# A linear-attention and GEGLU block on one core: M's high part and a chunk's parts of q in places that lie idle in the second pass, the sum of phi(k) by two fp32r products, and an order of instructions searched anew

## The chip, the cores and the metric

The kernel runs on one core of one Trainium2 chip. The core has five engines that work side by side: TensorE (PE, with its weight loads shown as PEld), VectorE (DVE), ScalarE (ACT), GpSimd (POOL) and SyncE (SP), which issues the transfers (DMA). Each engine takes its own instructions strictly in the order in which they were written down for it, and waits where an operand is not there yet. The metric is the time of one execution in device microseconds, where less is better.

## The reference

With x of 2048 rows (tokens) and 512 columns, 32 heads of 16 columns, and F = 1792:

```python
xn = layernorm(x)
q, k, v = xn @ wqkv, by heads
phi = lambda t: where(t > 0, t + 1, exp(t)) + 1e-6
kv  = einsum("bhsd,bhse->bhde", phi(k), v)
z   = einsum("bhsd->bhd", phi(k))                 # the sum of phi(k) over the tokens
o   = einsum(phi(q), kv) / (einsum(phi(q), z) + 1e-6)
s   = o @ wo
g   = silu((gelu(xn @ w_gate) * (xn @ w_up)) @ w_down)
out = x + s * g
```

All inputs and outputs are fp32.

## The kernel before

**Arithmetic.** An fp32 operand is split into a high part, rounded to the type fp32r, and a low part, which is the rest (`split`, L644: ACT casts the high part, DVE subtracts). A product of two split matrices is then three TensorE products, high by high, high by low and low by high (`three`, L671). The large matrix products are also taken apart by the Strassen-Winograd scheme: seven products of half-size blocks, gathered in three PSUM banks X, Y and Z. Product 1 is made in X and copied to Y by ACT (the "seed"), product 2 is added to Y; products 6, 7 and 4 are added to X, products 5 and 3 to Z. Between two of them a bank is saved or read by ACT or DVE, so a product has to wait until the one before it has been copied. Such a place, where PE makes a product, ACT copies it and PE goes on from the copy, is called a hand-over below. Almost every TensorE instruction is a 128x128 by 128x512 matmul that passes through one line, L665.

**Stages.** The tokens form four chunks of 512, taken in the order 2, 3, 0, 1.

- First stage, some 135 us: layernorm of 16 blocks of x, their transposes (`pt`, L866), the products for k and q (`k`, `q`, `X`, `Y`, `Z`), phi(k), its product with xn (`gps`), and its sum over the tokens (`zacc`, added up on POOL). k, q and phi are turned and spilled to DRAM.
- Then the sum of phi(k) over the partitions of `zacc` (`pz`, L1149, one fp32 product with a matrix of ones, named blk in the profile), kv (L1203) and the matrix M = kv times wo for all heads (L1210), which goes to DRAM as a high and a low part (`m_d`).
- The gated part runs in two passes over the weights, 28 weight tiles `w` each: pass 1 for the tokens of chunks 2 and 3, pass 0 (the second) for chunks 0 and 1. A weight tile gives three banks `FX`, `FY`, `FZ` (`quad`); their results go through gelu and the product with the up part into `h` and its split parts `hfh`, `hfl`; the down product gathers in banks `dX`, `dY`, `dZ` (`down_strassen`) and is added to `acc`. In the second pass the weight tiles come back from DRAM (1792 KB each) into three places of a ring (`ring("w", ...)`).
- At the turn from the first pass to the second, near 345 us, the attention products of chunk 2 are made (`sps`) and put aside in DRAM (`s_d`), silu is taken of the four first-pass sums, the tokens' split parts `Xh` and `Xl` are exchanged (14 transfers of 512 KB), and the weight tiles of the second pass begin to come in.
- End: the products of phi(q) with M for chunk 3 (the first end chunk, mixed with the last down products), then of chunks 0 and 1 (`sps`), the product with silu(g), the sum with x, and the transfers out.

**Where M and phi(q) lie at the end.** `load_m` takes two places of the weight ring, M0 (high) and M1 (low), 1024 KB each, when the weight tiles there are done with. phi(q) comes from DRAM into the places of `Xh` and `Xl` (the pool "xf", halves named pqh and pql): chunk 3 into pql, chunk 0 into pqh, chunk 1 into pql again. For chunk 3 the high and low parts were already split and stored (`t_d`, `tl_d`), so 8 transfers of 256 KB bring them in. pql becomes free when the last product of the last weight tile that reads `Xl` is done.

**The order.** The program is first noted down as operations with their costs and their predecessors (class `Plan`). TensorE's operations have a rough order, a list of keys (`pe_keys`), from which they may step ahead by 6 us at most. `Plan.order` (L309) then gives every operation a time by which it has to be done (`late`); `forward` (L440) runs through a model of the engines, and at each step gives an engine the ready operation with the lowest `late`. What comes out is the order of each engine's queue, for all five engines. Before, `late` comes from eight rounds of a backward reckoning (`latest`), followed by a list of random alterations that were kept (`KEPT`, `altered`).

Matmuls of 512 columns follow each other at a steady step when nothing is waited for; the rows of the prediction show it.

Of the kernel before, what the change touches and what calls it, by code (L numbers as in the profile page):

```python
# [18 lines left out]
KEPT = [  # L19
    (55, 70, [720000004]),  # L20
    (115, 135, [720000005]),
    (200, 270, [720000009]),
    (500, 560, [720000027]),
    (-1, 12, [720000035]),
    (70, 85, [720000040]),
    (-1, 12, [720000043]),
    (25, 40, [720000085, 720000134]),
    (200, 270, [720000140]),
    (-1, 12, [720000144]),
    (200, 270, [720000152]),  # L30
    (340, 420, [720000172, 720000184]),
    (100, 115, [720000203]),
    (340, 420, [720000233]),
    (500, 560, [720000243]),
    (40, 55, [720000247]),
    (560, 605, [720000257]),
    (200, 270, [720000279]),
    (340, 420, [720000290]),
    (500, 560, [720000362]),
    (200, 270, [720000390]),  # L40
    (55, 70, [720000517]),
    (40, 55, [720000540]),
    (340, 420, [720000555]),
    (270, 340, [720000602, 720000649, 720000655]),
    (340, 420, [720000658]),
    (270, 340, [720000690]),
    (500, 560, [720000887]),
    (12, 25, [720000899]),
    (55, 70, [720000957]),
    (500, 560, [720000974]),  # L50
    (40, 55, [720001218]),
    (-1, 12, [720001311]),
    (25, 40, [720001456]),
    (115, 135, [720001543]),
    (40, 55, [720001818]),
    (25, 40, [720001887]),
    (85, 100, [720001895]),
    (135, 200, [720001949]),
    (340, 420, [720002052]),
    (500, 560, [720002094]),  # L60
    (115, 135, [720002310]),
    (100, 115, [720002326]),
    (500, 560, [720002367]),
    (135, 200, [720002396]),
    (40, 55, [720002422]),
    (270, 340, [720002472]),
    (200, 270, [720002488]),
    (55, 70, [720002565, 720002605]),
    (115, 135, [720002669]),
    (100, 115, [720002694]),  # L70
    (55, 70, [720002734]),
    (40, 55, [720002796]),
    (100, 115, [720002858]),
    (40, 55, [720002901]),
    (340, 420, [720002982]),
    (70, 85, [720003200]),
    (420, 500, [720003430]),
    (-1, 12, [720003440]),
    (40, 55, [720003709, 720003813]),
    (70, 85, [720003981]),  # L80
    (115, 135, [720004064]),
    (25, 40, [720004170]),
    (100, 115, [720004402]),
    (500, 560, [720004624, 720004745]),
    (420, 500, [720004920]),
    (340, 420, [720005018]),
    (420, 500, [720005191]),
    (500, 560, [720005291]),
    (340, 420, [720005364]),
    (270, 340, [720005386]),  # L90
    (500, 560, [720005573]),
    (270, 340, [720005617]),
    (500, 560, [720005700, 720005753, 720005812]),
    (70, 85, [720005857]),
    (100, 115, [720005876, 720006137]),
    (200, 270, [720006523]),
    (340, 420, [720006542]),
    (270, 340, [720006565]),
    (500, 560, [720006740]),
    (270, 340, [720006762]),  # L100
    (420, 500, [720006797]),
    (100, 115, [720006937]),
    (25, 40, [720007069]),
    (100, 115, [720007820]),
    (270, 340, [720007916]),
    (200, 270, [720007997]),
    (100, 115, [720008028]),
    (40, 55, [720008434]),
    (70, 85, [720008559]),
    (40, 55, [720008706]),  # L110
    (55, 70, [720008751]),
    (-1, 12, [720008785, 720010301]),
    (25, 40, [720011151]),
    (-1, 12, [720011236]),
    (500, 560, [720011560]),
    (340, 420, [720011716]),
    (270, 340, [720011832]),
    (55, 70, [720011869, 720011995]),
    (40, 55, [720012578, 720013114]),
    (135, 200, [720013435]),  # L120
    (12, 25, [720013929]),
    (270, 340, [720014337]),
    (70, 85, [720015269]),
    (340, 420, [720015275]),
    (12, 25, [720015459]),
    (340, 420, [720016007]),
    (55, 70, [720016730]),
    (100, 115, [720016972]),
    (40, 55, [720017118]),
    (420, 500, [720019299, 720019742]),  # L130
    (25, 40, [720023341]),
    (560, 605, [720025689]),
    (200, 270, [720026707, 720027204]),
    (500, 560, [720027907]),
    (200, 270, [720029093]),
    (270, 340, [720029251]),
    (200, 270, [720030011]),
    (135, 200, [720030869]),
    (500, 560, [720031562]),
    (25, 40, [720032237]),  # L140
    (70, 85, [720033404]),
    (500, 560, [720034357]),
    (70, 85, [720034379]),
    (55, 70, [720034598]),
    (135, 200, [720037606]),
    (70, 85, [720037790, 720038397]),
    (200, 270, [720038864, 720039585]),
    (270, 340, [720041466]),
    (340, 420, [720041524]),
    (270, 340, [720041782]),  # L150
    (340, 420, [720043687]),
    (270, 340, [720043952]),
    (500, 560, [720044378]),
    (420, 500, [720044730]),
    (500, 560, [720044844]),
    (55, 70, [720045169]),
    (340, 420, [720045191]),
    (500, 560, [720045753]),
    (420, 500, [720045914]),
    (40, 55, [720046385]),  # L160
    (270, 340, [720047033]),
    (500, 560, [720047485]),
    (340, 420, [720048926]),
    (500, 560, [720049727]),
    (340, 420, [720050930, 720051286]),
    (500, 560, [720053709]),
    (420, 500, [720054380]),
    (70, 85, [720054716]),
    (135, 200, [720055100]),
    (500, 560, [720057087, 720057360, 720057458, 720057584, 720058015, 720058243]),  # L170
    (70, 85, [720058559]),
    (500, 560, [720059111, 720061740, 720062259]),
    (420, 500, [720065756]),
    (500, 560, [720067854, 720081154, 720082022]),
    (340, 420, [720085320]),
    (500, 560, [720089253]),
    (200, 270, [720097314]),
    (500, 560, [720110408, 720110529, 720112057, 720115333]),
    (200, 270, [720127077]),
    (420, 500, [720127080]),  # L180
    (40, 55, [720140141, 720140280, 720140297, 720140482]),
    (115, 135, [720140633]),
    (55, 70, [720141777]),
    (100, 115, [720141903]),
    (40, 55, [720144894]),
    (25, 40, [720146503]),
    (55, 70, [720146889]),
    (70, 85, [720147845]),
    (40, 55, [720149073]),
    (55, 70, [720163394, 720163465, 720163560, 720163641, 720163851]),  # L190
    (270, 340, [720165618]),
    (500, 560, [720168148, 720168524, 720169268, 720170070, 720170695]),
    (25, 40, [720171786]),
    (500, 560, [720172318]),
# [65 lines left out]
class Plan:  # L260
# [48 lines left out]
    def order(self, pe_keys):  # L309
        rank = {k: i for i, k in enumerate(pe_keys)}  # L310
        pe = sorted((o for o in self.ops if o.eng == "PE"), key=lambda o: rank[o.key])
        now = 0.0
        for o in pe:
            o.turn = now
            now += o.cost
        best = None
        done = self.ops_in_turn(pe)

        for n in range(8):
            self.latest(done, now, capacity=n > 0)  # L320
            done = self.forward(pe)
            end = max(t for t, _ in done)
            if best is None or end < best[0]:
                best = end, done, {o: o.late for o in self.ops}
# [7 lines left out]
    def altered(self, n, lo, hi, pe, _, done, late):  # L332
        draw = random.Random(n)
        for o in self.ops:
            o.late = late[o]
        waits = [w for w in self.waits(done) if lo <= w[0] < hi]
        if not waits or draw.random() < 0.3:
            waits += [(o.turn, 0.1, o) for o in pe if lo <= o.turn < hi]
        if not waits:
            return _, done, late  # L340
        w = draw.choices(waits, [w[1] for w in waits])[0]
        if draw.random() < 0.5:
            for o in self.chain(done, w[2]):
                if draw.random() < 0.7:
                    o.late -= draw.uniform(0.0, 4.0)
        else:
            at, back = w[2].late, draw.uniform(1.0, 12.0)
            share, far = draw.choice((1, 2, 3, 0.05, 0.2, 0.5)), draw.uniform(0.2, 4.0)
            near = [o for o in self.ops if at - back < o.late < at + 2.0]
            for o in draw.sample(near, min(len(near), share)) if share >= 1 else near:  # L350
                if share >= 1 or draw.random() < share:
                    o.late += draw.uniform(-far, far)
# [16 lines left out]
    def chain(self, done, o):  # L369
# [9 lines left out]
        for _ in range(14):  # L379
# [4 lines left out]
            if not held:  # L384
                break
# [1260 lines left out]
```

## Time and profile before

| | |
|---|---|
| median of 3 runs | 602.98 us (602.73 to 603.38) |
| the profiled execution's own time | 602.79 us |
| its span | 601.1 us |
| PE busy | 593.4 us (99%), 2626 matmuls |
| PEld (weight loads) busy | 481.2 us (80%) |
| DVE, ACT, POOL busy | 83%, 61%, 40% |
| granted TensorE clock | full in every slice |
| DMA | 141.27 MB, mean 235 GB/s |

The profiled execution is 0.19 us below the median, and its span is 1.69 us shorter than its time. A profile row gives a start in us from the span's start, a duration, the engine, the line, the operation, out<-in, and how many instructions the row stands for; square brackets hold the idle time of the engine ahead of the row and what ended it. The ends of matmuls are modelled, so PE looks busy in a row longer than a matmul's step; what a matmul really takes is read from the starts of those that follow.

### The profile page before, as it was taken

The page shows a single profiled execution, that of the slowest core. Times are in us where ns is not written, and L with a number is a line of the kernel's source. Part 1 is how long each engine was busy: PE and PEld are TensorE (multiplying, and loading weights), DVE is VectorE, ACT ScalarE, POOL GpSimd, SP SyncE. Part 2 cuts the span into 40 slices and gives each one's busy share as a digit, 9 for nine tenths or more (in the row PEclk, how much of TensorE's full clock was granted, in tenths as well). Part 3 has the DMA queues.
Part 4 walks back from the last instruction along what each step waited for, and adds up shares of the span by engine and source line. Part 5 has one row for each costly group of instructions (what it writes and reads, how often), then busy time and mean ns, then how long its engine had stood idle before and what let it go on. Part 6 is the DMA issues. An engine that isn't in the chain of part 4 may idle for free.

```text
span 601.1 us, 7826 instructions
## 1 busy us (share of the span) xinstructions
PE 593.4 (99%) x2626; PEld 481.2 (80%) x2626; DVE 499.3 (83%) x768; ACT 367.4 (61%) x663; POOL 242.0 (40%) x237
## 2 busy tenths in 40 slices
PE   8999999999999999999999999999999999999997
PEld 6887788777878888888887788888888888887786
DVE  6999988988788989999877675757698889898887
ACT  6687778877677765655545469567454544545620
POOL 4455856847636763605043730521122221206000
PEclk9999999999999999999999999999999999999999
DMA  7149977758986245467975899944656566648967
GB/s 271 46 131 281 287 229 237 235 186 275 379 314 226 91 158 209 158 210 299 336 231 184 323 393 381 332 163 140 210 174 210 175 228 201 218 156 269 364 219 269
DMA packets 78807, 141.27 MB, mean 235 GB/s; under 512 B 4656, under 2 KB 47664, under 8 KB 74672
## 3 DMA queue, kind: packets, MB, share of 16 engines
q1 hardware_dynamic: 78768, 140.79, 67.9%
q8 instruction: 20, 0.33, 0.2%
q14 instruction: 19, 0.16, 0.1%
HBM read 87.82 MB, written 52.95 MB: 234 GB/s over the span
## 4 chain that ended last, share of the span: by engine, by line
PE 85%; DVE 6%; DMA 6%; issue 1%; ACT 1%; SPq 0%; ACTq 0%; DVEq 0%
PE FX L665 25%; PE FZ L665 13%; PE dX L665 12%; PE FY L665 6%; PE gps L665 6%; PE dY L665 6%; PE X L665 4%; PE dZ L665 3%; DMA g<-g_d 2%; PE Z L665 2%; PE q L665 2%; PE sps L665 2%; PE k L665 2%; DMA pqh<-t_d 1%; PE Y L665 1%
## 5 line engine op out<-in xcount | busy, mean ns | idle before, releaser
L665 PE MATMUL FX<-Xh,w 128*128 128x512 f32 x448 | 134.7, 391 | 0.0
L1374 POOL TENSOR_TENSOR h<-h,g 128x512 f32<-128x512 f32 x28 | 38.9, 1390 | 150.5 <-DVE h L638 150.2
L665 PEld LDWEIGHTS FX<-Xh,w 128*128 128x128 f32 x448 | 83.9, 188 | 18.2 <-ACT fu L632 0.4
L665 PE MATMUL FX<-Xl,w 128*128 128x512 f32 x224 | 68.8, 389 | 0.0
L665 PE MATMUL FZ<-Xh,w 128*128 128x512 f32 x224 | 68.3, 391 | 0.0
L632 ACT COPY fu<-FX 128x512 f32<-128x512 f32 x56 | 32.9, 587 | 45.7 <-PE FX L665 43.2
L632 ACT COPY dY<-dX 128x512 f32<-128x512 f32 x56 | 32.0, 571 | 40.0 <-DVE acc L1328 30.6
L632 ACT CAST hfh<-sums 128x512 fp32r<-128x512 f32 x56 | 34.7, 622 | 27.9 <-DVE sums L638 27.7
L665 PEld LDWEIGHTS FZ<-Xh,w 128*128 128x128 f32 x224 | 42.0, 188 | 9.2 <-issue 0.5
L665 PEld LDWEIGHTS FX<-Xl,w 128*128 128x128 f32 x224 | 42.0, 188 | 8.8
L665 PE MATMUL dX<-hfh,dh 128*128 128x512 f32 x112 | 43.8, 395 | 0.3 <-ACT dY L632 0.3
L665 PE MATMUL dX<-hfl,dh 128*128 128x512 f32 x112 | 43.6, 391 | 0.0
L638 POOL TENSOR_TENSOR tmp<-raw 128x256 f32<-128x256 f32 x28 | 24.6, 886 | 47.2 <-ACT fu L632 24.1
L665 PE MATMUL dX<-hfh,dl 128*128 128x512 f32 x112 | 43.5, 390 | 0.0
L1328 DVE TENSOR_TENSOR acc<-acc,dX 128x512 f32<-128x512 f32 x48 | 32.9, 685 | 11.3 <-PE dX L665 10.7
L638 DVE TENSOR_TENSOR hfl<-sums,hfh 128x512 fp32r<-128x512 f32 x56 | 39.9, 721 | 2.5 <-ACT hfh L632 1.7
L1328 DVE TENSOR_TENSOR acc<-acc,dY 128x512 f32<-128x512 f32 x48 | 32.8, 684 | 10.8 <-PE dY L665 10.6
L638 POOL TENSOR_TENSOR sums<-draw 128x256 f32<-128x256 f32 x28 | 23.5, 850 | 34.9 <-DMA draw<-in_B_w_down 26.1
L638 DVE TENSOR_TENSOR hfl<-h,hfh 128x512 fp32r<-128x512 f32 x42 | 34.1, 817 | 1.6 <-ACT hfh L632 1.6
L638 DVE TENSOR_TENSOR h<-fu,FZ 128x512 f32<-128x512 f32 x28 | 19.2, 687 | 18.4 <-ACT fu L632 13.3
L665 PE MATMUL FY<-Xh,w 128*128 128x512 f32 x112 | 34.5, 390 | 0.0
L665 PE MATMUL FZ<-Xl,w 128*128 128x512 f32 x112 | 34.3, 389 | 0.0
(205 smaller groups left out, 1513.5 us busy)
## 6 DMA issues: line engine op xcount, KB each, us to landing
w<-w_d SPq DMA_DIRECT2D x17, 1792.0 KB, 7.9
w_d<-w SPq DMA_DIRECT2D x11, 1792.0 KB, 8.1
draw<-in_B_w_down SPq DMA_DIRECT2D x14, 512.0 KB, 6.4
w_d<-we SPq DMA_DIRECT2D x18, 256.0 KB, 2.1
x<-in_A_x SPq DMA_DIRECT2D x16, 256.0 KB, 4.5
q_d<-qp SPq DMA_DIRECT2D x16, 256.0 KB, 3.0
qz<-q_d SPq DMA_DIRECT2D x16, 256.0 KB, 3.7
q<-q_d SPq DMA_DIRECT2D x16, 256.0 KB, 3.9
```

The lines of the kernel that those rows point to most:

```text
L632: do("ACT", act(n, src.psum), lambda o, i: nc.scalar.copy(o, i), dst, src, name=name)
L638: do(eng, c, lambda o, p, q: getattr(e, f"tensor_{op}")(o, p, q), dst, a, b, name=name)
L665: nc.tensor.matmul(o if r is None else o[:, r], a, b, start=first, stop=made == self.passes[r], skip_group_check=self.on or r is not None)
L1328: do("DVE", dve(D), lambda o, i: nc.vector.tensor_add(o, o, i), o, ps, name="acc")
L1374: do("POOL", pool(NC), lambda o, i: nc.gpsimd.tensor_mul(o, o, i), h, g, name="h")
```

## The change

The change has four parts.

1. The sum of phi(k). `zacc` is split into two fp32r parts (an ACT cast and a DVE subtraction, 128x512 each), the matrix of ones is cast to fp32r once (128x128, ACT, at the very start), and `pz` is made of two fp32r products, ones by z's high part and ones by its low part, in place of one fp32 product.
2. M's high part. `load_m_early` takes it as two tiles Mh of 512 KB in the places R0 and R1 of the pool "rawp", which held raw weights and phi(q) of chunk 2 in the first pass and nothing in the second. The two transfers stand at the turn of the passes. The low part (Ml, 1024 KB) stays in the weight ring, one place of the ring earlier.
3. The parts of phi(q) of chunk 3. Seven of the eight go into one place of the weight ring (`pqw`), the eighth into a small idle tile (`pqt`, the place TMP of "rawp"). Chunk 0 takes the whole of pql, chunk 1 the whole of pqh.
4. The order. `latest`, `altered` and `KEPT` are gone; `late` is a table of numbers, one per operation (`LATE`), and `forward` makes the order from it as before.

```diff
-KEPT = [
-    (55, 70, [720000004]),
...
+LATE = [
+    -22047, 38, -946, 3475, -22738, -54555, -46091, -264, -48805, 868, 403, 695, 109, 1778, 1311, 1344, 1773, 1633, 154,
...
@@ Plan.order
-        best = None
-        done = self.ops_in_turn(pe)
-        for n in range(8):
-            self.latest(done, now, capacity=n > 0)
-            done = self.forward(pe)
...
-        for lo, hi, draws in KEPT:
-            for n in draws:
-                best = self.altered(n, lo, hi, pe, *best)
-        return [o for _, o in best[1]]
+        for o, late in zip(self.ops, LATE, strict=True):
+            o.late, o.lat0 = late / 100, o.lat
+        return [o for _, o in self.forward(pe)]
...
     pz = bank(7, "pz")
-    do("PE", 0.9, lambda o, a, b: nc.tensor.matmul(o, a, b, start=True, stop=True), pz, ones, zacc, key="z")
+    ones_r = tile_in("sm", "onr", [P, P], F32R, "ones_r")
+    do("ACT", 0.2, lambda o, i: nc.scalar.copy(o, i), ones_r, ones, name="ones")
+    zs = [tile_in("up", n, [P, D], F32R, f"z{n}") for n in (29, 32)]
+    split(*zs, zacc, D, "z")
+    def run_z(o, a, *zs):
+        for n, z in enumerate(zs):
+            nc.tensor.matmul(o, a, z, start=n == 0, stop=n == 1)
+    do("PE", 2 * PASS, run_z, pz, ones_r, *zs, key="z")
...
-            M.append(m)
+            M.append(lambda k, rows, m=m: m[:, k, rows])
         return M
+    def load_m_early():
+        high = [tile_in("rawp", r, [P, 2, D], F32R, f"Mh{r}") for r in (R0, R1)]
+        for r, m in enumerate(high):
+            src = View([m_d(k, ()).res[0] for k in (2 * r, 2 * r + 1)], m_d(0, (0, slice(None), slice(2 * r, 2 * r + 2))).get)
+            dma(m.map(lambda ap: ap.bitcast(F32)), src, 512)
+        low = tile_in("wp", ring("w", [0, 1, 2]), [P, KT, D], F32R, "Ml")
+        src = View([m_d(KT + k, ()).res[0] for k in range(KT)], m_d(KT, 1).get)
+        dma(low.map(lambda ap: ap.bitcast(F32)), src, 1024)
+        return [lambda k, rows: high[k // 2][:, k % 2, rows], lambda k, rows: low[:, k, rows]]
...
     keys, wait = ffn(0, moved)
-    M = load_m()
+    M = load_m_early()
+    pq = [tile_in("wp", ring("w", [0, 1, 2]), [P, 7, D], F32R, "pqw", 7), tile_in("rawp", TMP, [P, 2, D], F32R, "pqt", 1)]
     vs = {hl: tile_in("xf", hl, [P, 14, NC], F32R, f"pq{hl}", 14) for hl in "lh"}
...
-    for c, hl in zip(CHUNKS[1:], "lhl"):
+    attn(CHUNKS[1], M, lambda i, n: pq[(i - KT) // 7].part(
+        pq[(i - KT) // 7].res[(i - KT) % 7:(i - KT) % 7 + 1], (slice(None), slice((i - KT) % 7, (i - KT) % 7 + 1))))
+    for c, hl in zip(CHUNKS[2:], "lh"):
         attn(c, M, lambda i, n, v=vs[hl]: v.part(v.res[i:i + n], (slice(None), slice(i, i + n))))
```

How the rows stand in the queues, at three places. A row has the line, the operation, out<-in with each tile's number, the shape, and the count of equal instructions in a row (x4). The line numbers of the changed kernel are lower, since code was taken out ahead: L513 is there what L628 is before (the DMA issue), and L550 what L665 is (the matmul).

The SP queue (DMA issues) at the end, before: `M_5301` is M's low part, `draw` a raw down weight, `pql` the parts of phi(q) of chunk 3 from `t_d` (high) and `tl_d` (low), then `pqh` of chunk 0, `sxr` x for the last sum, `g` the silu of a first-pass sum, `s` what was put aside of chunk 2.

```order
L628 DMA sxr_5223<-in_A_xT 128x512
L628 DMA t_d<-sums_3674 128x4x128
L628 DMA draw_6_5284<-in_B_w_down 128x2x512
L628 DMA M_5301<-m_d 128x2048
L628 DMA s_5322<-s_d 128x512
L628 DMA g_5346<-g_d 128x512
L628 DMA g_5358<-g_d 128x512
L628 DMA pql<-t_d 128x512 x4
L628 DMA pql<-tl_d 128x512 x4
L628 DMA pqh<-t_d 128x4x512
L628 DMA s_5406<-s_d 128x512
```

And after:

```order
L513 DMA t_d<-sums_3702 128x4x128 x2
L513 DMA Ml<-m_d 128x2048
L513 DMA sxr_5248<-in_A_xT 128x512
L513 DMA draw_6_5276<-in_B_w_down 128x2x512
L513 DMA pqw<-t_d 128x512 x4
L513 DMA pqw<-tl_d 128x512 x3
L513 DMA s_5346<-s_d 128x512
L513 DMA g_5368<-g_d 128x512
L513 DMA g_5379<-g_d 128x512
L513 DMA s_5395<-s_d 128x512
L513 DMA pqh<-t_d 128x4x512
```

Here `pqh` is of chunk 1. The seven pieces for chunk 3 now stand right behind the last raw down weight, ahead of `s` and both `g`; the eighth (`pqt`) was issued some twenty rows earlier.

The same queue at the turn of the passes, before: `w_3451`, `w_3635` and `w_3657` are the second pass's first three weight tiles, numbered w14, w15 and w16 below, `so` the products of chunk 2 that are put aside, `qz` blocks of phi(q).

```order
L628 DMA Xh_3458<-xh_d 128x1024 x7
L628 DMA s_d<-so_3520 128x512
L628 DMA s_d<-so_3585 128x512
L628 DMA draw_0_3600<-in_B_w_down 128x2x512
L628 DMA qz_3603<-q_d 128x512
L628 DMA s_d<-so_3614 128x512
L628 DMA w_3635<-w_d 128x3584
L628 DMA Xl_3436<-xl_d 128x1024 x3
L628 DMA w_3657<-w_d 128x3584
L628 DMA Xl_3436<-xl_d 128x1024
```

And after:

```order
L513 DMA Xh_3473<-xh_d 128x1024 x7
L513 DMA Mh_3501<-m_d 128x1024
L513 DMA Mh_3510<-m_d 128x1024
L513 DMA qz_3556<-q_d 128x512
L513 DMA s_d<-so_3559 128x512
L513 DMA draw_0_3595<-in_B_w_down 128x2x512
L513 DMA s_d<-so_3620 128x512
L513 DMA w_3651<-w_d 128x3584
L513 DMA Xl_3444<-xl_d 128x1024 x3
L513 DMA w_3673<-w_d 128x3584
L513 DMA Xl_3444<-xl_d 128x1024
```

The two pieces of M stand ahead of w15 and of the last four pieces of `Xl`; one `so` less does.

The TensorE queue at the first weight tile of the gated part, before: `FX_1559` is bank X, whose first product ends with the second row; ACT then copies it to `FY_1583`.

```order
L665 MATMUL FX_1559<-Xh_168,w_1503 128x512 x4
L665 MATMUL FX_1559<-Xl_188,w_1503 128x512 x2
L665 MATMUL gps_382<-pkh_1543,xnh_1415 128x512
L665 MATMUL gps_356<-pkh_1543,xnh_1415 128x512
L665 MATMUL gps_375<-pkh_1543,xnh_1415 128x512
L665 MATMUL gps_382<-pkl_1576,xnh_1415 128x512
L665 MATMUL gps_356<-pkl_1576,xnh_1415 128x512
L665 MATMUL FY_1583<-Xh_168,w_1503 128x512 x2
```

And after:

```order
L550 MATMUL FX_1574<-Xh_170,w_1522 128x512 x2
L550 MATMUL gps_385<-pkh_1514,xnl_1512 128x512
L550 MATMUL FX_1574<-Xl_181,w_1522 128x512 x2
L550 MATMUL FX_1574<-Xh_170,w_1522 128x512 x2
L550 MATMUL gps_396<-pkh_1514,xnl_1512 128x512
L550 MATMUL gps_372<-pkh_1514,xnl_1512 128x512
L550 MATMUL gps_378<-pkh_1514,xnl_1512 128x512
L550 MATMUL FY_1593<-Xl_181,w_1522 128x512 x2
```

Between the last product in `FX` and the first in `FY` stood five other products before, and three after.

More of the change, by code (lines that the diff above doesn't have):

```diff
@@ L1 @@
-import random
 from contextlib import ExitStack
@@ L18 @@
 EPS = 1e-6
-KEPT = [
-    (55, 70, [720000004]),
[L21 to L194, printed above, removed]
@@ L332, in altered @@
[L332 to L352, printed above, removed]
-        new = self.forward(pe)
-        return max(t for t, _ in new), new, {o: o.late for o in self.ops}
@@ L1500, in attn @@
                     ps = bank(ring("sps", [3, 4, 2, 0, 1]), f"sps{c}{n}{m}", (P, NC // 2))
-                    Sum(ps).add(("S", c, n, m), *three([[v[:, k, rows] for v in M] for k in range(KT)],
+                    Sum(ps).add(("S", c, n, m), *three([[m(k, rows) for m in M] for k in range(KT)],
                                                        [[v[:, cs] for v in f] for f in forms_]), name="S", cost=SHORT)
@@ L1506, in attn @@
             ps = bank(ring("sps", [3, 4, 2, 0, 1]), f"sps{c}{n}")
-            Sum(ps).add(("S", c, n), *three([[m[:, k, rows] for m in M] for k in range(KT)], forms_), name="S")
+            Sum(ps).add(("S", c, n), *three([[m(k, rows) for m in M] for k in range(KT)], forms_), name="S")
             if c == CHUNKS[0]:
```

75 lines of the change are left out of this document (removed), and 177 rows, old and new, of the table LATE.

## The prediction

> **What bounds the kernel now.** I read the page's busy times first, then the chain of work that ended last, then the waits of PE, and at last PE's rows in time order wherever a wait stood.
>
> ```profile
> PE 593.4 (99%) x2626; PEld 481.2 (80%) x2626; DVE 499.3 (83%) x768; ACT 367.4 (61%) x663; POOL 242.0 (40%) x237
> PE 85%; DVE 6%; DMA 6%; issue 1%; ACT 1%; SPq 0%; ACTq 0%; DVEq 0%
> PE sps L665 <- DMA pql<-tl_d: 0.7, 1, 0.7
> PE X L665 <- ACT u L632: 0.2, 1, 0.2
> ```
>
> PE is busy for 593.4 of 601.1 us and carries 85% of the chain; the largest wait that the table names in the long middle and end is 0.7 us. So the time is the sum of PE's products plus small holes. What a change saves is what it takes from the count or length of products, or from a hole. For the holes I need the step of a product without waits and the price of a late hand-over:
>
> ```profile
> 329.50 0.39 PE L665 MATMUL FX<-Xh,w 128*128 128x512 f32 x1
> 329.73 0.39 PE L665 MATMUL dZ<-hfl,dh 128*128 128x512 f32 x1
> 329.96 0.46 PE L665 MATMUL dY<-hfl,dh 128*128 128x512 f32 x1
> 330.26 0.39 PE L665 MATMUL dX<-hfl,dh 128*128 128x512 f32 x1
> 330.62 0.74 PE L665 MATMUL FX<-Xh,w 128*128 128x512 f32 x2
> ...
> 335.77 0.39 PE L665 MATMUL dX<-hfh,dh 128*128 128x512 f32 x1
> 336.45 0.50 PE L665 MATMUL dX<-hfh,dh 128*128 128x512 f32 x1 [0.29 <-ACT dY L632]
> 336.79 0.40 PE L665 MATMUL dX<-hfl,dh 128*128 128x512 f32 x1
> ```
>
> ```profile
> 329.99 0.59 ACT L632 COPY fu<-FX 128x512 f32<-128x512 f32 x1
> ```
>
> The first three rows lie 0.23 us apart: the step of a product. The row at 329.50 ends a product in FX, ACT copies it from 329.99 to 330.58, and FX goes on at 330.62. From the next issue (329.73) that is 0.89 us: a hand-over needs four products between (0.92), and here stood three. The hole was 330.62 - 330.26 - 0.23 = 0.13; the first step after a wait is longer too (336.45 to 336.79: 0.34, so 0.11 more). A place with three products thus costs about 0.25 us.
>
> **The end (M and phi(q) in idle places).**
>
> ```profile
> 540.50 0.62 PE L665 MATMUL FZ<-Xh,w 128*128 128x512 f32 x2
> ...
> 546.85 0.62 PE L665 MATMUL FX<-Xl,w 128*128 128x512 f32 x2
> ...
> 550.44 0.50 PE L665 MATMUL dY<-hfh,dl 128*128 128x512 f32 x1
> ...
> 553.47 1.20 PE L665 MATMUL sps<-pql,M 128*128 128x512 f32 x4
> 554.51 0.40 PE L665 MATMUL dY<-hfh,dh 128*128 128x512 f32 x1
> ...
> 555.88 0.39 PE L665 MATMUL dZ<-hfh,dh 128*128 128x512 f32 x1
> 556.24 0.73 PE L665 MATMUL sps<-pql,M 128*128 128x512 f32 x2
> 557.67 0.50 PE L665 MATMUL sps<-pql,M 128*128 128x512 f32 x1 [0.70 <-DMA pql<-tl_d]
> ```
>
> ```profile
> 547.51 1.81 SPq L628 DMA_DIRECT2D pql<-t_d x4
> 549.36 2.35 SPq L628 DMA_DIRECT2D pql<-tl_d x4
> ```
>
> pql is free after the row at 546.85, its eight transfers go out from 547.51, and PE overtakes them: the four products at 553.47 take 1.04 instead of 0.92 (0.12), the step from 555.88 is 0.13 too long and the next 0.11, then comes the hole ahead of 557.67 (556.24 + 0.34 + 0.23 = 556.81, so 0.86) and its long step (0.11). Together 1.33 us. In the change seven of the eight pieces go where weight tile w26 was, which is free after the row at 540.50, some 6.4 us sooner. They then have from 541.0 until PE's place of the first of these products, which the new order has where the row at 550.44 is. Before, the eight took from 547.51 to 557.67 at most, 1.27 us a piece; seven at that pace end at 549.9, ahead of 550.44. I take the whole 1.33 as gone. Bounds: 0.3 stays if one piece is late; nothing is gained if the last raw down weight and Ml, which stand ahead of them in SP's queue, hold them for 6.4 us. M's low part is first read five microseconds later than the high part, and one place of the ring earlier; I cost it at nothing, covered by those products. The 1 MB of M's high part no longer crosses in the second pass's last part, which only relieves DMA there.
>
> **The sum of phi(k).**
>
> ```profile
> 147.62 1.02 PE L1149 MATMUL pz<-zacc,blk 128*128 128x512 f32 x2
> 148.07 1.03 PE L665 MATMUL FX<-Xh,w 128*128 128x512 f32 x2
> 148.95 0.62 PE L665 MATMUL FX<-Xl,w 128*128 128x512 f32 x2
> ```
>
> The fp32 product is two records; from 147.62 to 148.95 lie these and two FX products, so pz takes 1.33 - 2 x 0.23 = 0.87 us. Two fp32r products are 0.46: a gain of 0.41. The split adds one ACT cast and one DVE subtraction ahead of it, which hide behind the FX products that surround it (if that cover were gone, both would stall PE: 1.2 lost, twice the copy of 0.59). The cast of ones, a quarter of that copy's width, stands in ACT's queue ahead of everything, before any input is there; it costs nothing.
>
> **The order, start and first stage.**
>
> ```profile
> 8.39 0.50 PE L665 MATMUL k<-kq,Xh 128*128 128x512 f32 x1
> 8.92 0.51 PE L665 MATMUL k<-kq,Xl 128*128 128x512 f32 x1
> 9.47 0.50 PE L665 MATMUL k<-kq,b 128*128 128x512 f32 x1
> ...
> 14.00:67.00 53.00, 52.18 (x238) 41.21 (x237) 49.62 (x83) 40.87 (x75) 30.71 (x28) 1.00 0.60 174
> ...
> 51.33 0.39 PE L665 MATMUL gps<-pkh,xnh 128*128 128x512 f32 x1
> 51.81 0.66 PE L866 MATMUL pt<-blk,xn 128*128 128x128 f32 x4
> ```
>
> Three holes stand in the first k products (0.30 ahead of 8.92, 0.32 ahead of 9.47, and 0.11 in the long step after it). The new order takes the first product with b six places later, behind products whose operands come first, so that its hole goes; I take 0.30, between 0 (DVE is busy 49.6 of 53 us from 14 to 67, and may only hand the wait on) and 0.73. The transposes at 51.81 come 0.25 late (0.10 more in their own steps): there 8 products stood since the transposes that filled the other bank, now 13 do: 0.35 gained. One hand-over of the third group (X3, the u row of the waits) has three products now instead of two: 0.23.
>
> **The order, gated and down products.** I counted the products between the two ends of every hand-over in both orders. Two that waited get a fourth product: the one at 330.62 (0.25) and the one at 336.45 (hole 0.45 and 0.11 after, of which I take 0.40, since its ACT copy came late for another reason too). Seven that had four to ten have three now (in the first stage two, then FX0, FX2, FX14, FX27 to their next product, and one of the down products): 7 x 0.25 = 1.75 lost. Bounds: 0, if the order makes PE wait there where it would wait later anyway, and 3.5, if ACT starts as late as at 336.45.
>
> **The turn of the passes.**
>
> ```profile
> 360.00:375.00 15.00, 15.00 (x67) 12.22 (x66) 8.47 (x14) 14.29 (x22) 0.83 (x2) 1.00 0.98 384
> ...
> 361.29 0.59 ACT L632 COPY dY<-dX 128x512 f32<-128x512 f32 x1
> 361.90 1.28 ACT L1288 ACT_TABLE_LOAD   x1
> 363.20 0.60 ACT L1288 ACTIVATE g<-FY 128x512 f32<-128x512 f32 x1
> ...
> w<-w_d SPq DMA_DIRECT2D x5, 1792.0 KB, 9.7
> ```
>
> ```profile
> 353.37 0.32 SPq L628 DMA_DIRECT2D w<-w_d x1
> 364.46 0.61 PE L665 MATMUL FX<-Xh,w 128*128 128x512 f32 x2
> ```
>
> Two loads are new on a busy path. The two 512 KB pieces of M go ahead of w15 in a stretch where DMA is full (0.98 of its engines, 384 GB/s): 1 MB there is 2.7 us, less 0.7 for the one `so` of 256 KB that now stands behind. w15 went out at 353.37 and with the median of 9.7 us landed near 363.1; first used at 364.46. Two microseconds later would be 365.1 against a first use that the new order puts near 364.9. And the order switches between silu and gelu eight times here instead of six: two table loads more, 1.28 us each, on an ACT that is 14.29 of 15 us busy. Since ACT is free enough on both sides of that stretch, and the copies for which PE waits are moved up between the loads, I take 0.1 lost, bounds 0 and 2.6.
>
> The Trainium skill weighs against the change here: "ScalarE: Activation LUTs", What ACT_TABLE_LOAD costs, gives about 1.28 us for the load and 1.38 more for a drain, 2.66 a switch. The trace agrees with the first and not with the second: the copy ahead ends at 361.88, the load stands at 361.90, and the activation starts at 363.20.
>
> **The sum.** -1.33 (end) - 0.41 (pz) - 0.30 (start) - 0.35 (transposes) - 0.23 (X3) - 0.25 - 0.40 (two hand-overs) + 1.75 (seven hand-overs) + 0.1 (turn) = -1.42 us. From the profiled 602.79 that is 601.37; the median lies 0.19 above the profiled execution, so 601.6.
>
> **Rivals.**
>
> 1. *Tight hand-overs decide; slower.* In the second half of the order 36 hand-overs have five products or fewer between, before 17. Five are 1.14 us, enough for 0.89, but not if ACT is behind by one copy of 0.59: then 0.34 are short, and with the 0.11 some 0.45 is lost at each. The new order for this would have to leave ACT one instruction late at six of the 29 not yet counted (2.7 us over the forecast: 604.3); at nine, 605.6. For it: 336.45, where ACT came late. Against: ACT is busy 61% and few of the 17 waited.
> 2. *ACT at the turn.* 14.29 + 2 x 1.28 = 16.85 in 15 us; if nothing can move out of the stretch, PE waits 1.85 instead of 0.1: 603.4. For it: the 95%. Against: copies for PE can pass in front.
> 3. *ACT at the turn with a drain at each switch.* If ACT, at each of the two added switches, stood still for as long again as its load, it would need 14.29 + 4 x 1.28 = 19.4 in 15 us, and PE would wait 4.4: 605.9. Against: the rows at 361.29 to 363.20 leave no such gap. The rule of the Trainium skill ("ScalarE: Activation LUTs", What ACT_TABLE_LOAD costs), weighed above, would make it so.
> 4. *The pieces for chunk 3 come late all the same.* Held behind Ml and the raw down weight, the hole at the end returns: 601.6 + 1.33 = 602.9, no change.
>
> **Chances and range.** A difference of under 0.2% (601.77 to 604.19) can't be told from no change here. Forecast 0.62, itself 599.6 to 602.4 (0.48 faster, 0.14 same); rival 1 0.14 (slower); rival 2 0.12 and rival 4 0.10 (same); rival 3 0.02 (slower). So faster 0.48, same 0.36, slower 0.16. The range is 599.6 to 604.6: below lies 0.06, when the seven cost nothing (599.8) and the start gives its whole 0.73; above 0.12, most of rival 1.
>
> **What would show it.** End: no idle ahead of `sps` on `pqw`, and the first of these products near 549. pz: two rows of 0.23 a step. The hand-overs: FY after FX0 and FX2 with a wait on ACT. The turn: PE full in 360 to 375 with ACT above 95%, and no wait for w15. The forecast is wrong if DVE in the first stage lets new holes open, since every queue is rewritten and only the places above were priced.

## The result and the profile after

Over 19 runs each, the changed kernel takes 601.71 us in the median (601.07 to 602.76) and the kernel before 602.71 us (601.78 to 604.25). The medians differ by 1.0 us; the ratio is 0.998, with a 95% interval of 0.9974 to 0.9986, or 0.8 to 1.6 us less. It is a real gain, and as small as the 0.2% that was named as the bound of what can be told from no change. The profiled execution has a span of 599.4 us against 601.1.

The page after, busy times, then the shares of the chain that ended last:

```profile
PE 592.2 (99%) x2626; PEld 481.0 (80%) x2626; DVE 504.6 (84%) x769; ACT 372.9 (62%) x667; POOL 250.8 (42%) x237
PE 95%; DVE 2%; DMA 1%; ACT 0%; SPq 0%; issue 0%; ACTq 0%; DVEq 0%
```

The count of matmuls is as before, and PE now carries 95% of the chain instead of 85%: DMA and DVE, 6% each before, make 1% and 2% of it. From the table of PE's waits after, the first three behind the opening:

```profile
PE k L550 <- ACT kq L517: 0.7, 1, 0.7
PE dX L550 <- DVE acc L1221: 0.4, 2, 0.2
PE dX L550 <- ACT dY L517: 0.2, 1, 0.2
```

The wait of `sps` for pql is gone; the largest one is now in the first k products. The sum of phi(k), in PE's rows after, in time order:

```profile
147.29 0.62 PE L550 MATMUL FX<-Xh,w 128*128 128x512 f32 x2
147.75 0.62 PE L1041 MATMUL pz<-z,ones_r 128*128 128x512 f32 x2
148.21 0.63 PE L550 MATMUL FZ<-Xh,w 128*128 128x512 f32 x2
```

Two fp32r products take 148.21 - 147.75 = 0.46 us, where the fp32 product took 0.87. The end, PE's rows and the transfers for chunk 3 on SP:

```profile
549.51 0.40 PE L550 MATMUL dX<-hfl,dh 128*128 128x512 f32 x1
549.75 0.86 PE L550 MATMUL sps<-pqw,Mh 128*128 128x512 f32 x3
550.44 0.40 PE L550 MATMUL sps<-pqt,Mh 128*128 128x512 f32 x1
550.68 1.07 PE L550 MATMUL sps<-pqw,Mh 128*128 128x512 f32 x4
```

```profile
539.64 2.24 SPq L513 DMA_DIRECT2D pqw<-t_d  x4
541.92 1.38 SPq L513 DMA_DIRECT2D pqw<-tl_d  x3
```

And from the view of the tile pqw after, how long its transfers took:

```profile
DMA to landing us min/median/max: 2.6/6.0/6.6
```

The seven pieces go out from 539.64, 7.9 us sooner than before, and the eight first products of chunk 3 follow each other from 549.75 without a hole. The last piece is issued at 542.87 and lands 6.6 us later, near 549.5, a quarter of a microsecond ahead of PE.

To see where the time went I lined up the two traces by the work that PE had done: for each matmul the sum of the steps of all that come ahead of it (0.227 us for 512 columns, and pz left out), and then the difference of the start times at equal sums. Changes of this difference are gains and losses at that place. At the times of the kernel before, after minus before in us:

```
  5.9   39.5   50.6   63.4   74.2  108.0  120.0  143.5  155.4  176   323.6
+0.08  +0.13  +0.49  -0.42  -0.66  -0.68  -1.00  -1.24  -1.67  -1.46  -1.50
335.5  347.5  359.0  393.6  438.9  541.0  552.8  565.7  588.6
-1.25  -1.28  -0.77  -1.14  -1.02  -0.83  -0.94  -1.88  -1.92
```

Read downwards: nothing at the start, 0.4 lost by 50.6 and 1.7 gained from there to 144 (1.4 in the first stage as a whole), 0.4 at pz, nothing in 150 us of the first pass, 0.7 lost around the turn, 0.4 won back at 390, 0.3 lost again by 541, and 0.9 to 1.1 gained at the end. These are two executions. The changed kernel's profiled one took 601.16 us, 0.55 less than its median, and the sum of 1.9 is therefore more than the 1.0 us of the medians; some 0.5 of that lies in the first stage, as is shown further down.

### The profile page after: what moved, and what is told of

Same layout as the page of the kernel before. It is cut to its first block, busy times and chain, and to the rows that moved or that the text cites. A ratio compares the mean times of both kernels' runs of the same rounds, so it can differ in the third digit from the quotient of the medians.

```text
span 599.4 us, 7871 instructions
## 1 busy us (share of the span) xinstructions
PE 592.2 (99%) x2626; PEld 481.0 (80%) x2626; DVE 504.6 (84%) x769; ACT 372.9 (62%) x667; POOL 250.8 (42%) x237
## 4 chain that ended last, share of the span: by engine, by line
PE 95%; DVE 2%; DMA 1%; ACT 0%; SPq 0%; issue 0%; ACTq 0%; DVEq 0%
PE FX L550 26%; PE FZ L550 13%; PE dX L550 12%; PE gps L550 7%; PE sps L550 7%; PE FY L550 6%; PE dY L550 6%; PE X L550 5%; PE dZ L550 3%; PE Z L550 2%; PE k L550 2%; PE q L550 2%; PE Y L550 1%; DMA wk<-in_A_wqkv 1%; PE pt L751 1%; DVE acc L1221 1%
## 5 line engine op out<-in xcount | busy, mean ns | idle before, releaser
L550 PE MATMUL FX<-Xh,w 128*128 128x512 f32 x448 | 130.3, 391 | 0.1
L550 PEld LDWEIGHTS FX<-Xh,w 128*128 128x128 f32 x448 | 83.7, 188 | 19.0 <-ACT fu L517 0.6
L550 PE MATMUL FX<-Xl,w 128*128 128x512 f32 x224 | 68.0, 391 | 0.0
L550 PE MATMUL FZ<-Xh,w 128*128 128x512 f32 x224 | 67.8, 391 | 0.0
L550 PEld LDWEIGHTS FZ<-Xh,w 128*128 128x128 f32 x224 | 42.0, 188 | 9.3 <-issue 0.5
L550 PEld LDWEIGHTS FX<-Xl,w 128*128 128x128 f32 x224 | 41.8, 188 | 9.1 <-ACT fu L517 0.6
L550 PE MATMUL dX<-hfl,dh 128*128 128x512 f32 x112 | 43.7, 392 | 0.5 <-DVE acc L1221 0.2
L550 PE MATMUL dX<-hfh,dh 128*128 128x512 f32 x112 | 43.3, 394 | 0.2 <-DVE acc L1221 0.2
L523 DVE TENSOR_TENSOR hfl<-sums,hfh 128x512 fp32r<-128x512 f32 x56 | 41.6, 755 | 2.1 <-ACT hfh L517 1.5
L550 PE MATMUL dX<-hfh,dl 128*128 128x512 f32 x112 | 43.0, 390 | 0.0
L1068 POOL TENSOR_TENSOR qz<-qz,zq 128x512 f32<-128x512 f32 x16 | 24.3, 1518 | 43.4 <-DMA qz<-q_d 41.0
L523 POOL TENSOR_TENSOR tmp<-raw 128x256 f32<-128x256 f32 x28 | 27.0, 975 | 36.0 <-DVE w L523 26.4
L517 ACT CAST hfh<-h 128x512 fp32r<-128x512 f32 x42 | 26.1, 620 | 20.7 <-DVE h L523 10.9
L550 PE MATMUL FY<-Xh,w 128*128 128x512 f32 x112 | 34.7, 394 | 0.0
```

Of the source, the lines that this page charges most:

```text
L517: do("ACT", act(n, src.psum), lambda o, i: nc.scalar.copy(o, i), dst, src, name=name)
L523: do(eng, c, lambda o, p, q: getattr(e, f"tensor_{op}")(o, p, q), dst, a, b, name=name)
L550: nc.tensor.matmul(o if r is None else o[:, r], a, b, start=first, stop=made == self.passes[r], skip_group_check=self.on or r is not None)
L1068: do("POOL", pool(D), lambda o, z: nc.gpsimd.tensor_mul(o, o, z.unsqueeze(1).to_broadcast([P, KT, P])), rows_of(q), zq, name="u")
```

## The experiments

All of them state the order of every queue as a list of operations, so that one row can be moved and all the others stay. Line numbers are therefore others again (L472 is the matmul, L439 ACT's copy, L435 the DMA issue).

**The parts without the new order.** The changed places and the two products for pz, in the order of the kernel before.

```diff
 (order of the kernel before, all five queues)
+ACT   ones_r <- blk                 first
+ACT   z high, DVE z low             where zacc is ready
-PE    pz <- zacc,blk
+PE    pz <- z,ones_r (two)
-SP    M (high), 1024 KB             at 526.6
+SP    Mh, 512 KB, twice             behind the seven Xh loads
+SP    Ml, 1024 KB                   at 526.6
-SP    M (low)                       at 540.7
-SP    pql <- t_d x4, tl_d x4        at 547.5
+SP    pqw <- t_d x4, tl_d x3        at 540.7
+SP    pqt <- tl_d                   at 472
```

> The changed kernel's places for M and phi(q) and its two-product sum of phi(k), but every queue in the order of the kernel before (only the added or moved instructions are put in: the cast of ones first on ACT, z's split where zacc is ready, Mh behind the seven Xh loads, the seven pieces of phi(q) where M's low part was loaded). Theory: these two parts carry the gain, 0.41 us at pz and 1.1 to 1.3 at the end, so 1.5 to 1.7 us less than before, ratio 0.997 to 0.9975; the first stage and 325 to 360 us stay as before. Rival (the new order carries the gain): under 0.5 us gained, since the early pieces and Mh push other transfers in the old order and new waits open at the turn or the end.

Measured: 601.99 us, ratio 0.9979 (0.9971 to 0.9988), not to be told from the changed kernel's. Against the trace of before the difference is flat from 17 to 140 us, falls by 0.43 at pz, is flat to 549 (no loss at the turn from the Mh transfers), and falls by 0.93 by 561 and 1.1 by 582. PE's rows of this kernel at the end, in time order:

```profile
555.45 1.09 PE L472 MATMUL sps<-pqw,Mh 128*128 128x512 f32 x4
556.37 0.39 PE L472 MATMUL dZ<-hfh,dh 128*128 128x512 f32 x1
556.60 0.84 PE L472 MATMUL sps<-pqw,Mh 128*128 128x512 f32 x3
557.28 0.39 PE L472 MATMUL sps<-pqt,Mh 128*128 128x512 f32 x1
```

No hole is left where 0.86 us stood. But PE now comes sooner to a down product whose operand DVE has ready no sooner than before (the second `hfl` ends at 557.95), and a hole of 0.26 opens there that wasn't in the kernel before, with 0.11 in the long step behind it. PE's rows:

```profile
557.51 0.39 PE L472 MATMUL dZ<-hfl,dh 128*128 128x512 f32 x1
558.00 0.50 PE L472 MATMUL dX<-hfl,dh 128*128 128x512 f32 x1
558.34 0.39 PE L472 MATMUL dX<-hfh,dl 128*128 128x512 f32 x1
```

That leaves 1.33 - 0.37 = 0.96 us of the hole's price, which is what the lined-up traces show by 561. So the two small parts are the gain, and the new order as a whole adds nothing that the times show (by the two intervals, to within some 0.6 us): it gains 0.8 between 56 and 67 us and loses nearly as much at the turn. The profiled execution started late (1.1 us behind before's at 17 us, with the queues the same but for the cast of ones), on which more is said at the end.

**How much room the pieces have.** One transfer moved in SP's queue of the changed kernel.

```diff
 SP  draw_6 <- in_B_w_down
+SP  s <- s_d
 SP  pqw <- t_d x4
 SP  pqw <- tl_d x3
-SP  s <- s_d
 SP  g <- g_d
```

> The changed kernel with one transfer of 256 KB (a block put aside of chunk 2) issued ahead of the seven pieces for chunk 3 instead of behind them. In the changed kernel the last piece lands at 549.46 and PE reads the first at 549.75. Theory (the pieces come just in time): they land about 0.65 later, and PE waits 0.2 to 0.5 us at the first products of chunk 3. Rival (the place was free so early that there is room): no wait at all, the end as in the changed kernel.

SP's rows of this kernel around the moved transfer, and below them PE's at the first products of chunk 3:

```profile
543.04 0.33 SPq L435 DMA_DIRECT2D s<-s_d  x1
543.42 1.85 SPq L435 DMA_DIRECT2D pqw<-t_d  x4
```

```profile
549.94 0.39 PE L472 MATMUL dX<-hfl,dh 128*128 128x512 f32 x1
551.98 1.04 PE L472 MATMUL sps<-pqw,Mh 128*128 128x512 f32 x3 [1.65 <-DMA pqw<-tl_d]
```

PE waits 1.8 us, and 2.0 are lost by 559 against the changed kernel, in this one execution: more than either theory. The reason is in the first row: the moved transfer itself could only go out at 543.04, when its own destination was free (a DVE product, `h`, ends at 543.01), and SP takes its queue in order, so the seven pieces behind it went out at 543.42 instead of 539.64. The run therefore doesn't measure what 256 KB ahead of the pieces cost. The room that the pieces have is read from the landing above, a quarter of a microsecond; what a place in SP's queue costs is set by the row ahead of it, not by its 256 KB.

**One more product in each tight hand-over.** Nine places of the changed kernel, as here at 137 us:

```diff
 PE  FX <- Xh,w            (two)
-PE  gps <- pkh,xnl
 PE  FX <- Xl,w            (two)
 PE  FX <- Xh,w            (two)   the seed's last product
 PE  gps <- pkh,xnl        (three)
+PE  gps <- pkh,xnl
 PE  FY <- Xl,w            (two)
```

> The changed kernel with one or two independent products moved into the gap of nine hand-overs at which PE waited (42.9, 50.6, 57.3, 61.0, 80.3, 104.4, 120.1, 137.2 and 544.6 us); nothing else is moved. Theory: a hand-over with three products costs about 0.25 us and with four nothing, so each place gives back its hole and the long step behind it, 0.24 to 0.46, together 2.0 to 2.6 us against the changed kernel; ratio to the kernel before about 0.994. Rival (the wait only moves to the next hand-over, because ACT and DVE set the pace there): under 1 us in all.

PE's rows at this place in the changed kernel, and then in the one with four products between:

```profile
136.36 0.84 PE L550 MATMUL gps<-pkh,xnl 128*128 128x512 f32 x3
137.18 0.73 PE L550 MATMUL FY<-Xl,w 128*128 128x512 f32 x2
```

```profile
136.34 1.07 PE L472 MATMUL gps<-pkh,xnl 128*128 128x512 f32 x4
137.25 0.65 PE L472 MATMUL FY<-Xl,w 128*128 128x512 f32 x2
```

In the first, three steps of 0.227 would end at 137.04; FY starts 0.14 later. In the second, four end at 137.25, where FY starts. All nine holes are gone: the price of a hand-over is right, 0.25 us with three products and next to nothing with four. The whole is not: 601.22 us, ratio 0.9967 (0.9955 to 0.9979), some 0.8 us better than the changed kernel by the ratios, whose intervals overlap, where 2.0 to 2.6 were expected. That is the size which the rival named, that of a wait that only moves. New holes have opened, at transposes that now come too early for DVE. PE's rows at the largest:

```profile
64.66 0.62 PE L472 MATMUL X<-kq,Xh 128*128 128x512 f32 x2
66.07 0.66 PE L673 MATMUL pt<-blk,xn 128*128 128x128 f32 x4 [0.79 <-DVE Xl L445]
```

The three products that were moved up had stood between two groups of transposes, and there they had covered a wait for a bank. Others of 0.2 to 0.3 us are at 51.8, 63.3, 82.9 and, behind the last of the nine places, 545.3. At 562 a down product waits 0.9 us for ACT, which stands at a cast. ACT's rows:

```profile
559.29 0.62 ACT L439 CAST pql<-pql 128x512 fp32r<-128x512 f32 x1 [1.77 <-DMA pql<-t_d]
559.82 0.61 ACT L439 CAST hfh<-sums 128x512 fp32r<-128x512 f32 x1
560.34 0.61 ACT L439 CAST pql<-pql 128x512 fp32r<-128x512 f32 x1
560.86 0.61 ACT L439 CAST hfh<-sums 128x512 fp32r<-128x512 f32 x1
561.38 0.58 ACT L439 COPY dY<-dX 128x512 f32<-128x512 f32 x1
```

The seed of dY stands four rows behind a cast of chunk 0's phi(q), whose transfer was late in this execution.

**Four more places.**

```diff
 at 334  PE  dX <- hfh,dh ... dY <- hfh,dl
+        PE  FZ <- Xh,w (two)     from ahead of them
         PE  dX x3
+        PE  FX <- Xh,w (two)     from ahead of them
         DVE acc dX, acc dY
+        DVE h <- fu,FZ                                     from ahead of them
 at 354 +PE  dY <- hfh,dl; dX <- hfl,dh
         PE  FX <- Xh,w (weight tile 14)
 at 564 +PE  dY x3
         PE  dX x3 (waits for DVE)
 start  +SP  wk (third)
         SP  x5
        +PE  k x2, k <- Xl (operands there)
         PE  k (waits for ACT)
```

> As the kernel with covered hand-overs, and four more places: at 334 us four products of the last gated tile and one DVE sum are moved behind the down products whose bank they held up; at 354 two down products go ahead of the first product of weight tile 14, at 563.8 three down products go ahead of the one that waits for DVE; at the start the third block of wk is loaded ahead of x5 again, as in the kernel before, and three products that are ready go ahead of the one that waited for it. Theory: these give 1.0, 0.34, 0.4 and 0 to 0.4 us more, so 1.6 to 2.1 less than the kernel with covered hand-overs, ratio to the kernel before about 0.991. Rival: the later products make the next stage wait (the split of h at 335, the last down products), and half of it or less is gained.

Measured: 600.5 us, ratio 0.9961 (0.9949 to 0.9974), some 0.4 us less than the step before and, with these intervals, not to be told from it. The rival was nearer: the holes at 334, 354 and 564 are gone, but 0.56 us opens at 335.3 (a DVE sum behind the h of the moved product) and 0.2 at the seed of FY behind 354, and the wait at 561 (0.66) stays. At the start nothing is gained: the hole goes from 9 us to 10.5, because ACT now waits 0.62 us for the fourth block of wk instead of 0.47 for the third in the changed kernel.

**The waits that showed next.**

```diff
 PE   three groups of transposes two to five products later (51.8, 65.5, 82.1)
 PE   one product, or two, more in the hand-overs at 220.2, 329.4 and 356.3
 DVE  acc dX ahead of h <- g,FX (335)
 ACT  seed of dY ahead of two casts pql <- pql (560)
 (the change at the start left out)
```

> The kernel with covered hand-overs and moved groups (its change at the start left out), with the waits that showed next there covered in the same way: three groups of transposes go two or three products later (51.8, 65.5, 82.1 us), the hand-overs at 220.2, 329.4 and 356.3 get one or two products more, at 335.3 a DVE sum goes ahead of a gated one, and at the end ACT copies the seed of dY before the two casts of chunk 0's phi(q) that wait for a transfer. Theory: each wait of PE is a local matter of order, so these give 0.25 + 0.7 + 0.16 + 0.25 + 0.25 + 0.3 + 0.56 + 0.65 = 3.1 us against the kernel before it in the series, and the ratio to the kernel before comes to about 0.991. Rival: DVE sets the pace of the first stage, the waits for the transposes come back a few us later, and only the end (0.65 to 0.9) and the turn (0.5) are gained: ratio 0.994.

Measured: 598.64 us (598.30 to 599.06), ratio 0.9927 (0.9913 to 0.9941), 4 us better than the kernel before and 2 better than the step ahead of it. That lies between the two theories. The first stage did not fall back: with the transposes later, 1.2 us are gained there against the changed kernel. The largest that is left in the table of PE's waits:

```profile
PE dX L472 <- ACT dY L439: 1.1, 2, 0.7
```

These two, 0.9 at 359.8 and 0.5 at 339.4, are new and behind moved products at the turn. They weren't taken on.

**Table loads at the turn, fewer and more.**

```diff
 fewer:  ACT  -silu (374.0)  ... gelu, gelu  +silu  silu, silu
 more:   ACT  gelu (376.3) ... +silu  gelu (377.7) ... -silu
```

> The changed kernel with one silu at the turn moved behind the next gelus, to stand with two others, so that ACT loads its table six times there instead of eight. Theory (the two loads more lie beside PE's work): PE gains nothing from 357 to 392 us, within 0.1. Rival (they cost PE time): 0.3 to 1.9 us gained there.

> The changed kernel with one silu at the turn moved between two gelus, so that ACT loads its table ten times there instead of eight (2.6 us more on ACT at 377 us). ACT is busy 13.2 of 15 us from 375 to 390. Theory: ACT's copies for PE right behind (the save at 377.2, the seed at 378.6) come up to 3.2 us later and have 1 to 2 us of room, so here PE waits, 0.5 to 2 us. If a switch cost twice its load (with a drain), ACT's rows would show gaps of 1.3 us around each load and PE would wait 2.6 more.

With two loads fewer the run took 608.03 us, 6.4 us of it lost at one place. Of this kernel, SP's rows, PE's rows, and the busy times by engine of one window (PE, PEld, DVE, ACT, POOL, then the granted clock, the DMA share and GB/s):

```profile
370.09 11.49 SPq L435 DMA_DIRECT2D g_d<-acc  x3
381.70 0.36 SPq L435 DMA_DIRECT2D w<-w_d  x1
```

```profile
386.91 0.39 PE L472 MATMUL dX<-hfh,dl 128*128 128x512 f32 x1
390.78 2.90 PE L472 MATMUL FX<-Xh,w 128*128 128x512 f32 x6 [3.48 <-DMA w<-w_d]
393.47 1.06 PE L472 MATMUL FX<-Xl,w 128*128 128x512 f32 x2
```

```profile
390.00:396.50 6.50, 5.72 (x14) 4.55 (x15) 2.31 (x4) 1.60 (x3) 4.27 (x5) 0.50 1.03 420
```

The moved silu is stored to g_d; the store stands in SP's queue ahead of a weight tile, and so the tile went out at 381.70. SP's row in the changed kernel:

```profile
375.11 0.36 SPq L513 DMA_DIRECT2D w<-w_d  x1
```

From 357 to 386 us the difference to the changed kernel stays within 0.1, so the two loads that are gone had not been on PE's path; what the run really shows is that the silu's place sets when the next weight tile is fetched. The wait of 3.6 us cost another 2.7 behind it: for 13 steps PE ran at 0.43 us instead of 0.23, with a granted clock of 0.50 from 390 to 396.5.

With two loads more, ACT's rows, and below them PE's at the wait:

```profile
378.15 0.59 ACT L439 COPY fu<-FX 128x512 f32<-128x512 f32 x1 [0.33 <-ACT g L1103]
378.76 1.28 ACT L1370 ACT_TABLE_LOAD   x1
380.05 0.63 ACT L1370 ACTIVATE acc<-acc 128x512 f32<-128x512 f32 x1
380.71 1.28 ACT L1103 ACT_TABLE_LOAD   x1
382.00 0.63 ACT L1103 ACTIVATE g<-g 128x512 f32<-128x512 f32 x1
382.54 0.58 ACT L439 COPY FY<-FX 128x512 f32<-128x512 f32 x1
```

```profile
383.17 0.73 PE L472 MATMUL FX<-Xh,w 128*128 128x512 f32 x2 [2.27 <-ACT FY L439]
```

PE waits 2.4 us, a little more than expected. The seed of FY comes behind a silu and two loads, 3.2 us of ACT, and PE loses 2.6 of them. Each load is 1.28 us long, with the next activation 0.01 us behind it and a gap of 0.02 ahead. A switch so costs ACT its load alone, and PE as much of it as there is no room for; the two that the run before left out had cost PE nothing where they stood.

## Why the prediction was right, point by point

The time (601.6 forecast, 601.71 measured, or 1.4 us less against 0.8 to 1.6) is right, and so is its base, that PE's products and holes are the time. That it agrees to 0.1 us is luck: the medians differ by 1.0 us where the sum has 1.42, and the kernel before has 602.71 in the median of 19 where the forecast starts from 602.98. In the sum the two parts make -1.74 and the order +0.32. Term by term it is right for the two parts, one of them too large, and wrong in several terms of the order, whose errors cancelled.

- *The end, -1.33:* the mechanism is right, by the places alone, without the new order. The size is 0.9 to 1.1 (the changed kernel 0.94 by 565.7, the kernel with the parts alone 0.93 to 1.1). The holes of 1.33 are gone; what the sum left out are down products that PE now reaches before DVE is ready, for 0.37 at 558.0 in the kernel with the parts alone and for 0.48 at 563.8 in the changed kernel. The room was smaller than the 0.5 us that "seven at that pace end at 549.9, ahead of 550.44" left: the first products came at 549.75 and the last piece near 549.5. Rival 4 (the hole returns) is wrong for the order as it is, but one row ahead in SP's queue brings it back.
- *The sum of phi(k), -0.41:* right: 0.43 gained by the lined-up traces, and the two products take the 0.46 that were forecast.
- *The start, -0.30:* wrong. "The new order takes the first product with b six places later ... so that its hole goes": that hole went, and one of 0.88 took its place at 8.98, a k product that waits for ACT, and ACT for the third block of wk, which SP now issues behind x5. In five later executions with the same first k products it is 0.3 instead, and in most of them a second of 0.3 stands behind a few products later, so that the 0.30 isn't gained there either. Putting SP's and PE's rows back gained nothing. Nor could it be measured in one execution: four profiled executions with the same rows up to there (the changed kernel and the three with rows moved only later) differ at 17 us by up to 0.7.
- *Transposes, -0.35, and X3, -0.23:* right; the changed kernel has no hole at the transposes of 51.8, and X3's hand-over at 61.0 has 0.27 instead of 0.5.
- *What was not priced:* the seed of Y in the third group (0.37 and 0.11 at 57.8 before) and the transposes at 63.4 and 66.2 also improved, together some 0.7 us once a new hole of 0.46 at 57.3 is taken off. Some 0.5 of the gain by 120 is not the order's: in three later executions of the same rows X waits 0.6 for DVE at 118, which the profiled execution of the changed kernel doesn't.
- *Two hand-overs, -0.25 and -0.40:* the first is gone, but near it, at 329.3, FZ now waits for a DVE product, which takes as much (0.15 and 0.11). In the second place the new order put the fourth product in, and lost all the same. PE's rows after:

```profile
333.95 0.50 PE L550 MATMUL dX<-hfl,dh 128*128 128x512 f32 x1 [0.25 <-DVE acc L1221]
334.29 0.39 PE L550 MATMUL dX<-hfh,dl 128*128 128x512 f32 x1
334.52 0.40 PE L550 MATMUL dX<-hfh,dh 128*128 128x512 f32 x1
335.15 0.50 PE L550 MATMUL dX<-hfl,dh 128*128 128x512 f32 x1 [0.24 <-ACT dY L517]
```

  Two holes of 0.41 stand there with 0.11 behind each. At the first the bank was held by a DVE sum (`acc`) that had to let a gated product (`h`) pass; at the second ACT's copy came behind the next such sum. Counting products between PE's rows doesn't see that.
- *Seven hand-overs, +1.75:* the price of 0.25 is right (four of them waited 0.24 to 0.27: 50.6, 120.1, 137.2, 544.6), the count is not: the other three cost 0.1 to 0.15 or nothing, about 1.3 in all.
- *The turn, +0.1:* right as to the table loads, w15 and the last `Xl` pieces, for none of which PE waits. But 0.35 was lost at 354.18, where the first product of weight tile 14 waits for ACT to copy `so` out of the bank: a hand-over with three products that my count, of products in the same group of banks, had left out. In return the hole of 0.32 before at 390.45 is gone.
- *Rival 1 (tight hand-overs, slower)* did not decide: those with four or five products hardly waited (from 170 to 329 us only one place in PE's rows after waits, at 220, and loses under 0.2). *Rival 2 (ACT at the turn)*: in the changed kernel ACT is busy 12.46 us of 360 to 375, less than the 14.29 before, because the new order spreads the eight loads from 351 to 386 us; the "ACT above 95%" that was to show didn't come. The window by engine, after:

```profile
360.00:375.00 15.00, 15.00 (x68) 12.24 (x67) 6.63 (x11) 12.46 (x20) 1.30 (x1) 1.00 0.93 372
```

- *Rival 3 (a drain at each switch)* is refuted by every load, those of the run with ten included. The drain of 1.38 us that the Trainium skill gives in "ScalarE: Activation LUTs", What ACT_TABLE_LOAD costs, shows in none of these traces; its 1.28 us for the load show in all of them.

## What to carry to other kernels

When PE is busy throughout, price a new order by walking each late operand back through every engine that it passes, with that engine's own queue: counting the products that cover a hand-over gave the right price and missed the waits in which DVE or SP had another row first. Covering one hole with products taken from elsewhere pays only if they covered nothing there; the four microseconds below the kernel before came when the next waits were covered too. A transfer's place in SP's queue is worth what the row ahead of it waits for.

## What was not expected of the hardware

PE's clock fell to half in a wait: with 3.48 us of idle it ran 13 products at 0.43 us, and with 2.27 us of idle, in the run with more table loads, none. The Trainium skill, "TensorE: Matmul & The Clock Gate", What's actually happening, says that the clock is halved after an idle window of about 3.4 us. Here it fell sooner: the granted clock is still 1.00 from 389.0 to 389.5 and 0.50 from 389.8, some 2.4 us after the last product ahead of the wait ended in the trace (387.30). Two waits don't give a threshold. The wait of 3.6 us cost 6.4 in all.

The first matmuls are not repeatable: up to 0.7 us between executions of the same rows by 17 us, and 0.6 at 118. For the start the traces show where much of it comes from. PE begins with 24 products of 128x128 (`warm`), which step at 0.21 us at first and at 0.11 later. The change comes at 4.0 us in one execution and at 7.3 in another with the same rows, the runs with fewer and with more table loads:

```profile
1.11 4.28 PE L502 MATMUL warm<-blk 128*128 128x128 f32 x24 [1.11 <-DVE neg_half L494]
```

```profile
1.12 5.49 PE L502 MATMUL warm<-blk 128*128 128x128 f32 x24 [1.12 <-DVE neg_half L494]
```

Their first k products start at 7.22 and 7.92. The kernel with the parts alone also has the change at 7.3 and the first k product at 7.92, against 4.0 and 7.02 in the kernel before: most of its late start. A single profile can't weigh an edit of less than that in the first 120 us; from 140 to 325 us they agree within 0.2.
